# Delta rule and rational MLP on one core: one list of places for every engine and the DMA queue

## The chip, the cores and the metric

The kernel runs on one core of a Trainium2 chip. A core has five engines that run side by side and wait for each other by semaphores: TensorE (PE in the profile, its weight loads PEld), VectorE (DVE), ScalarE (ACT), GpSimd (POOL) and SyncE (SP), which here issues nearly all DMAs. The metric is the device time of one execution in microseconds (us); lower is better.

## The reference

A delta-rule recurrence over 768 steps in 4 batches x 8 heads of width 48 makes y, and a rational MLP is applied to each of its 3072 rows of 384.

```python
# attention: B, H, S, D = 4, 8, 768, 48
k_n = k / (norm(k) + 1e-6)
for t in range(S):
    y[:, :, t] = einsum('bhd,bhde->bhe', q[:, :, t], state)
    v_old = einsum('bhde,bhd->bhe', state, k_n[:, :, t])
    state += beta[:, :, t] * outer(k_n[:, :, t], v[:, :, t] - v_old)
# MLP: x = y as (3072, 384), w_in (384, 2048), w_out (2048, 384)
h = x @ w_in
P = a0 + a1*h + a2*h**2 + a3*h**3
Q = 1 + |b0|*|h| + |b1|*h**2
out = (P / (Q + 1e-6)) @ w_out
```

## The kernel before

**Chunks.** The 768 steps are cut into 12 chunks of 64 (`NCH`). For a chunk, *stages* written as Python generators do the attention: `load_k/q/v` fetch the inputs, `keys` normalizes and transposes k, `kbd` writes it by DMA into a block-diagonal tile, `gram` and `gl` form key products (`g`, sent to DRAM as `gd` and read back in blocks as `gb`), `inverse` inverts triangular blocks on VectorE (`wt`, then `wh`, sent out as `img` and read back as `wc`), `blocks` and `solve` finish the triangular solve (`et`, `ebd`, `wbd`, `pu`, `z`), `next` updates the state `S16`, `outputs` makes y, and `tokens` and `scalars` prepare the scaled rows `xT` and the table `msc` for the MLP. A `yield` ends a *step* of a stage.

**Units.** The MLP is cut into 96 units, 8 for a chunk (`NU`, 256 columns of the 2048 each): `hidden` (18 matmuls into `ph`, L902), `numerator`, `cubic` and `quotient` (six VectorE operations of 128 x 512, L926 to L953, five on ScalarE, one on GpSimd), and `accumulate` (12 matmuls into `po`, L969). The tiles `mx` of the units are a ring of three buffers. The first VectorE operation of `numerator` (L926) marks a unit below. Units 0 to 7 need chunk 0's tokens, units 8 to 15 need chunk 1's, and so on.

**Weights.** `load_in` and `load_out` (8 of each) fetch 768 KB of float64 words into a staging tile (`wsi`, `wso`) and turn them into float32 and then into two float16 parts: ScalarE (L343), GpSimd (L344), three VectorE operations (L345, L347 twice) and more. The staging tiles are of the same ring of three as `mx`, so that a weight's DMA waits until the weight three places earlier has been converted, and unit 0 waits until nearly all weights have been. The `units` 0 to 3 of chunk 0 use the first four weights of each kind, with a scalar table of their own; units 4 to 7 use the others.

**What sets the order.** Each step of a chunk has a time in units (`PLAN`), each step of a unit another (`UNIT`), the same for all chunks and units; the steps are sorted by time. Steps before unit 8 (`upto = 8.0`), the constants and the weights are written in groups (chunk 0, weights 0 to 3, weights 4 to 7, later chunks), and the framework's scheduler, with its own model of time, orders them on every engine. From unit 8 on VectorE, ScalarE, TensorE and GpSimd follow the sorted steps (`manual_schedule`); the SP queue is ordered by the scheduler throughout. Two things hold work back by hand: `gate`, a scalar that is made from the result of chunk 0's inverse (L631) and that the conversions of weights 4 to 7 and of all of `w_out` read on GpSimd (L344), and `BEHIND`, by which some loads are issued after a named DMA.

```python
        nc.gpsimd.tensor_scalar(t.bitcast(F32), t.bitcast(F32), 3.0e38, keep, op0=ALU.min, op1=ALU.max)   # L344, keep = gate
    if upto < N:
        with tc.manual_schedule(engines={DVE, Activation, PE, Pool}):   # L1142, names shortened
```

Of the kernel before, what the change touches and what calls it, by code (L numbers as in the profile page):

```python
# [36 lines left out]
def kernel(  # L37
# [16 lines left out]
    P = 128  # L54
# [39 lines left out]
    marks = {}  # L94
    BEHIND = {"k1": "kbd0", "v1": "kbd0", "q1": "gb0", "k2": "gb0", "v2": "gb0", "q2": "gb0", "knbd0": "gb0"}

    def mark(nm, c, dma):
        marks[f"{nm}{c}"] = dma.ins

    def behind(nm, c):  # L100
        after = marks.get(BEHIND.get(f"{nm}{c}"))
        return nullcontext() if after is None else tc.issue_after(after)

# [6 lines left out]
    for t in wide.values():  # L110
        nc.vector.memset(t[:, :, :, D:], 0.0)

    def load(nm, c):
        t = wide[nm] if nm in wide else sb.tile([P, HP, D], F32, tag="ld" + nm, name=f"{nm}_{c}", bufs=LD_BUFS[nm])
        with behind(nm, c):
            for b in range(2):
                sl, src = slice(b * C, (b + 1) * C), SRC[nm][:, :, c * C : (c + 1) * C]
                if nm == "v":
                    nc.sync.dma_start(out=t[sl], in_=src[2 * b : 2 * b + 2].rearrange("p h t d -> t (p h) d"))
                else:  # L120
                    for i in range(2):
                        nc.sync.dma_start(out=t[sl, :, i, :D], in_=src[2 * i + b].rearrange("h t d -> t h d"))
        loaded[nm, c] = t
# [21 lines left out]
    nc.gpsimd.memset(mask, 1.0 / 256.0)
    for b in range(2):
        sl = slice(b * C, (b + 1) * C)
        nc.gpsimd.affine_select(
            out=mask[sl],
            in_=mask[sl],  # L150
            pattern=[[1, C]],
            compare_op=ALU.is_gt,
            fill=0.0,
            base=0,
            channel_multiplier=-1,
        )
# [15 lines left out]
    bblk = cpool.tile([P, NCH, 16], F32, name="bblk")  # L172
    for j in range(NB):
        nc.scalar.dma_start(
            out=bblk[j:P:NB],
            in_=beta.rearrange("b h (c j i) -> j (b h) c i", j=NB, i=16)[j],
        )

    nc.gpsimd.tensor_scalar(bblk, bblk, 1.0 / 256.0, 0.0, op0=ALU.mult, op1=ALU.add)


    def zeroed(n, shape, dtype, nm, part=lambda t: t, eng=nc.gpsimd):
        made = []
# [24 lines left out]
    NIMG = 2
    img = []
    for i in range(NIMG):  # L210
        t = dfix.tile([P, BS], F32, name=f"img{i}")
        nc.scalar.dma_start(out=t, in_=zero)
        img.append(t)
# [82 lines left out]
    NU = NF // 2  # L296
    w_in = cpool.tile([P, NU, 2, NCC, 2 * P], F16, name="w_in")
# [9 lines left out]
    def tables(lo, hi):  # L307
# [3 lines left out]
        nc.scalar.activation(wn, wn, AF.Exp, scale=0.5, bias=consts[:, 1:2])  # L311
        row = [tab[:, i, u] for i in range(6)]
# [11 lines left out]
        nc.vector.tensor_scalar_mul(io, total(io, hi - lo, f"o{lo}", ps_h, "h"), 2.0 ** -14)  # L324
# [9 lines left out]
    gate = cpool.tile([P, 1], F32, name="gate")  # L334

    def to_f32(t, src, nm, keep=MIN_NORMAL):

        n = t.shape[-1]
        st = staged([P, n, 2], U32, "ws" + nm)
        parts_ = src.shape[1]  # L340
        nc.sync.dma_start(out=st.rearrange("p (a f) w -> p a (f w)", a=parts_), in_=src)
        wl, wh = st[..., 0], st[..., 1]
        nc.scalar.activation(t.bitcast(F32), wh.bitcast(F32), AF.Abs)  # L343
        nc.gpsimd.tensor_scalar(t.bitcast(F32), t.bitcast(F32), 3.0e38, keep, op0=ALU.min, op1=ALU.max)  # L344
        nc.vector.tensor_scalar(t, t, 3, KEEP, op0=ALU.logical_shift_left, op1=ALU.bitwise_and)  # L345
        for word, scalar, op0 in ((wh, 0xC0000000, ALU.bitwise_and), (wl, 29, ALU.logical_shift_right)):
            nc.vector.scalar_tensor_tensor(out=t, in0=word, scalar=scalar, in1=t, op0=op0, op1=ALU.bitwise_or)  # L347

    def load_in(i):
        w64 = moe_w_in.bitcast(U32)
        t = w_out[:, i].rearrange("p a b e -> p (a b e)").bitcast(U32)
        to_f32(
            t, w64[:, i * 4 * P : (i + 1) * 4 * P].rearrange("(c p) x -> p c x", p=P), f"i{i}", gate if i >= 4 else MIN_NORMAL
        )
        t = t.bitcast(F32).rearrange("p (c f) -> p c f", c=NCC)
        s2 = w_in[:, i, 0].bitcast(BF16)
        nc.scalar.activation(s2, t, AF.Square)
        pf = ps_h.tile([P, 2 * P], F32, tag="h", name=f"pfw{i}")  # L360
        for cc in range(NCC):
            nc.tensor.matmul(pf, ones16, s2[:, cc], start=cc == 0, stop=cc == NCC - 1)
        ss = sb.tile([P, 1], F32, tag="ss", name=f"wss_{i}")
        nc.vector.tensor_reduce(sw[:, 2, i : i + 1], pf, axis=AX.X, op=ALU.max)
        nc.vector.tensor_scalar_max(sw[:, 2, i : i + 1], sw[:, 2, i : i + 1], 2.0 ** -60)
        nc.scalar.activation(s2[:, 0], pf, AF.Copy, accum_out=ss)
        nc.vector.tensor_scalar_max(ss, ss, 2.0 ** -2)
        scale_of(sw[:, 0, i : i + 1], ss, f"w{i}")
        split16((w_in[:, i, 0], w_in[:, i, 1]), t, sw[:, 0, i : i + 1])

    def load_out(i):
# [5 lines left out]
        to_f32(t, w64[2 * i * P : (2 * i + 2) * P].rearrange("(j p) x -> p j x", j=2), f"o{i}", gate)  # L377
# [65 lines left out]
    def to_diagonal(nm, t, c=0):  # L443
        bd = diag[nm][c % len(diag[nm])]
        for b in range(2):
# [7 lines left out]
            elif nm in "kq":  # L453
                dma = nc.sync.dma_start(
# [3 lines left out]
                mark(nm + "bd", c, dma)  # L458
# [41 lines left out]
    info = {}  # L500
# [3 lines left out]
    def keys_normalized(c):  # L504

        nrm = sb.tile([P, 4, HP], F32, tag="nrm", name=f"nrm_{c}", bufs=1)
        kt = loaded.pop(("k", c))
# [21 lines left out]
        info[c] = {}  # L529
# [21 lines left out]
    def key_products(c):  # L551
# [3 lines left out]
        mm3(pg, d["kbd"], d.pop("tk"))  # L555
# [616 lines left out]
```

## Time and profile before

| | |
|---|---|
| median of 3 runs (lowest, highest) | 792.67 us (790.21, 793.26) |
| the profiled execution | 790.87 us, span 789.1 us, mean granted TensorE clock 0.925 |
| busy, share of the span | VectorE 712.7 us (90%), ScalarE 661.9 (84%), TensorE 639.4 (81%), GpSimd 313.9 (40%) |
| DMA | 84.35 MB, mean 107 GB/s |

The span runs from the first to the last instruction; 1.8 us of the execution lie around it. Busy time is that in which an engine has at least one operation under way; back-to-back VectorE operations overlap a little, so that the sum of their durations is more. Idle time before an operation is put down to what released it. Times in rows are microseconds from the start of the span. A row of windows gives a stretch, its length, then each engine's busy time in it with the number of instructions, the granted TensorE clock, the mean busy share of the 16 DMA engines and GB/s.

### The profile page before, as it was taken

The numbers are of one execution on the slowest core, as the hardware profiler recorded it, in microseconds if no ns is written. First come the engines' busy times: TensorE is split into PE (matmuls) and PEld (weight loads), VectorE is DVE, ScalarE is ACT, GpSimd is POOL, SyncE is SP. The second block draws the span as 40 slices with busy tenths as digits, with TensorE's granted clock in tenths as the row PEclk, the third lists the DMA queues.
The fourth block names the chain that finished last, engine by engine and source line by source line (L and its number), as shares of the span: only waits on it lengthen the run. The fifth ranks groups of instructions, "written<-read, shape, count | busy, mean of one in ns | idle before, by whom it ended". The sixth has DMA issues, their size and how long they took to land.

```text
span 789.1 us, 23451 instructions
## 1 busy us (share of the span) xinstructions
PE 639.4 (81%) x9520; PEld 510.7 (65%) x9520; DVE 712.7 (90%) x1290; ACT 661.9 (84%) x1301; POOL 313.9 (40%) x321
## 2 busy tenths in 40 slices
PE   0413555768599899899999998999999988999995
PEld 0313544657488778777687787777877876777662
DVE  5698789799679999999999999999999999898996
ACT  3765788988779999999999999999999977887973
POOL 7542356352125436335354353353442342222222
PEclk9955586799599999999999999999999999999999
DMA  8897897747836467286385574772853713400000
GB/s 230 189 187 188 190 197 148 121 82 122 131 61 118 82 120 136 57 151 117 67 146 110 99 132 82 132 135 43 162 95 77 137 26 55 85 2 22 1 21 21
DMA packets 358412, 84.35 MB, mean 107 GB/s; under 512 B 349856, under 2 KB 352928, under 8 KB 358304
## 3 DMA queue, kind: packets, MB, share of 16 engines
q1 hardware_dynamic: 356128, 81.69, 53.7%
q8 instruction: 75, 1.23, 0.7%
q10 hardware_dynamic: 2176, 1.17, 0.5%
q14 instruction: 33, 0.27, 0.1%
HBM read 34.70 MB, written 13.65 MB: 61 GB/s over the span
## 4 chain that ended last, share of the span: by engine, by line
DVE 41%; PE 20%; ACT 6%; DMA 3%; issue 3%; SPq 0%; POOLq 0%; ACTq 0%; DVEq 0%
PE ph L902 8%; DVE ph L951 5%; DVE mg L949 5%; DVE mx L953 4%; PE po L969 4%; DVE mx L936 4%; DVE mx L926 4%; DVE mx L934 4%; DVE z L257 3%; PE py L422 2%; ACT mx L923 2%; PE pm L422 1%; DMA gd<-g 1%; DVE pr L597 1%; DVE pr L616 1%
## 5 line engine op out<-in xcount | busy, mean ns | idle before, releaser
L955 POOL TENSOR_TENSOR mg<-mx 128x512 f16<-128x512 f32 x96 | 129.0, 1344 | 327.5 <-DVE mx L953 175.4
L969 PE MATMUL po<-w_out,mg 128*128 128x384 f16 x1152 | 218.0, 327 | 10.9 <-DVE mg L949 5.7
L902 PE MATMUL ph<-xT,w_in 128*128 128x256 f16 x1728 | 209.1, 276 | 12.2 <-DVE mx L953 8.6
L902 PEld LDWEIGHTS <-w_in 128*128 128x128 f16 x1728 | 167.4, 99 | 44.9 <-DVE mx L953 18.1
L969 PEld LDWEIGHTS <-mg 128*128 128x128 f16 x1152 | 106.3, 98 | 72.1 <-DVE mg L949 10.9
L922 ACT ACTIVATE mx<-ph,msc 128x512 f32<-128x512 f32 x96 | 65.5, 683 | 21.2 <-PE ph L902 19.0
L949 DVE SCALAR_TENSOR_TENSOR mg<-mx,msc 128x512 f16<-128x512 f32 x96 | 75.4, 785 | 1.3 <-ACT mx L945 1.2
L951 DVE SCALAR_TENSOR_TENSOR ph<-mx,msc,mg 128x512 f32<-128x512 f32 x96 | 73.8, 769 | 1.2
L422 PE MATMUL pu<-z,ebd 128*128 128x48 f16 x1728 | 54.3, 188 | 25.1 <-DVE z L257 20.3
L422 PEld LDWEIGHTS <-ebd 128*128 128x128 f16 x1728 | 53.8, 100 | 32.2 <-issue 29.8
L923 ACT ACTIVATE mx<-ph,coef,msc 128x512 f32<-128x512 f32 x96 | 74.4, 775 | 0.0
L422 PEld LDWEIGHTS <-kbd 128*128 128x128 f16 x1680 | 58.9, 103 | 21.9 <-issue 13.5
L953 DVE SCALAR_TENSOR_TENSOR mx<-mx,msc,ph 128x512 f32<-128x512 f32 x96 | 71.2, 742 | 1.6
L934 DVE TENSOR_TENSOR mx<-ph,mx 128x512 f32<-128x512 f32 x96 | 65.5, 682 | 6.4 <-ACT mx L923 6.2
L936 DVE SCALAR_TENSOR_TENSOR mx<-mx,msc,ph 128x512 f32<-128x512 f32 x96 | 71.0, 739 | 0.0
L926 DVE SCALAR_TENSOR_TENSOR mx<-mx,msc,ph 128x512 f32<-128x512 f32 x96 | 70.8, 738 | 0.0
L928 ACT ACTIVATE mx<-mx 128x512 f32<-128x512 f32 x96 | 60.1, 626 | 11.6 <-DVE mx L926 11.6
L943 ACT ACTIVATE mx<-mx,msc 128x512 f32<-128x512 f32 x96 | 68.7, 715 | 0.1
L945 ACT ACTIVATE mx<-mx 128x512 f32<-128x512 f32 x96 | 60.4, 629 | 2.2
L253 POOL TENSOR_TENSOR mm<-m,mm 128x512 f16<-128x512 f32 x24 | 33.9, 1419 | 28.4 <-ACT mm L247 19.2
L255 ACT ACTIVATE z<-pu,zmask 128x768 f16<-128x768 f32 x36 | 32.7, 910 | 11.3 <-PE pu L422 10.6
L422 PEld LDWEIGHTS <-wbd 128*128 128x128 f16 x1152 | 34.3, 99 | 11.0 <-issue 6.7
(197 smaller groups left out, 1228.9 us busy)
## 6 DMA issues: line engine op xcount, KB each, us to landing
wsi<-in_moe_w_in_dram SPq DMA_DIRECT2D x8, 768.0 KB, 7.7
gd<-g SPq DMA_DIRECT2D x24, 256.0 KB, 4.9
wso<-in_moe_w_out_dram SPq DMA_DIRECT2D x8, 768.0 KB, 5.8
mbd<-mm SPq DMA_DIRECT2D x24, 256.0 KB, 4.9
wc<-img SPq DMA_DIRECT2D x24, 256.0 KB, 4.8
wbd<-wc SPq DMA_DIRECT2D x24, 256.0 KB, 5.1
knbd<-kn SPq DMA_DIRECT2D x44, 128.0 KB, 4.3
kw<-in_k_dram SPq DMA_DIRECT2D x48, 96.0 KB, 3.4
```

The source lines that it names most:

```text
L422: nc.tensor.matmul(dst[p][:, h], head(bd, lp, p * H + h), head(rt, rp, p * H + h), start=start and n == 0 and h == 0, stop=stop and n == l ...
L902: nc.tensor.matmul(ph[:, i], w_in[:, f2, wp, cc, i * P : (i + 1) * P], x[:, xp, cc], start=k == 0, stop=k == 3 * NCC - 1,)
L923: nc.scalar.activation(u, ph, AF.Identity, scale=A3, bias=a2)
L926: in_order(nc.vector.scalar_tensor_tensor(out=w, in0=z, scalar=B0, in1=ph, op0=ALU.add, op1=ALU.mult))
L934: in_order(nc.vector.tensor_mul(u, ph, u))
L936: in_order(nc.vector.scalar_tensor_tensor(out=u, in0=u, scalar=A1, in1=ph, op0=ALU.add, op1=ALU.mult))
L943: nc.scalar.activation(r, w, AF.Ln, bias=Q0)
L949: in_order(nc.vector.scalar_tensor_tensor(out=g[:, 0], in0=u, scalar=A0, in1=r, op0=ALU.add, op1=ALU.mult))
L951: in_order(nc.vector.scalar_tensor_tensor(out=t, in0=w, scalar=Q0, in1=g[:, 0], op0=ALU.add, op1=ALU.mult))
L953: in_order(nc.vector.scalar_tensor_tensor(out=u, in0=u, scalar=A0, in1=t, op0=ALU.add, op1=ALU.subtract))
L955: nc.gpsimd.tensor_mul(g[:, 1], u, r)
L969: nc.tensor.matmul(po[p], g[:, gp, i, p * P : (p + 1) * P], w_out[:, f2, wp, i], start=f2 == lo and i == 0 and k == 0, stop=f2 == hi - 1 a ...
```

## The change

The table of times, the scheduler's part, the gate and `BEHIND` go. Every step of every stage, for each chunk, unit, weight, constant and zeroed buffer by itself, gets a place in one list of 2996 (`PLACES`); `run` walks the list once, and `manual_schedule()` without arguments makes all engines and the SP queue follow it. To this end the constants, the zeroing of buffers, the weights' conversion and the tables have become stages with steps of their own; `weights` i and the scalars of units 0 to 3 and 4 to 7 can stand anywhere among the chunks' steps. The arithmetic is the same, but for the gate's two operands and one constant tile (`ident16`) that nothing read.

```diff
-    BEHIND = {"k1": "kbd0", "v1": "kbd0", "q1": "gb0", "k2": "gb0", "v2": "gb0", "q2": "gb0", "knbd0": "gb0"}
...
-        with behind(nm, c):
-            for b in range(2):
+        for b in range(2):
...
-    gate = cpool.tile([P, 1], F32, name="gate")
-    def to_f32(t, src, nm, keep=MIN_NORMAL):
+    def to_f32(t, src, nm):
...
+        yield
         nc.scalar.activation(t.bitcast(F32), wh.bitcast(F32), AF.Abs)
-        nc.gpsimd.tensor_scalar(t.bitcast(F32), t.bitcast(F32), 3.0e38, keep, op0=ALU.min, op1=ALU.max)
+        yield
+        nc.gpsimd.tensor_scalar(t.bitcast(F32), t.bitcast(F32), 3.0e38, MIN_NORMAL, op0=ALU.min, op1=ALU.max)
+        yield
...
-        if c == 0:
-            nc.vector.tensor_scalar(
-                gate.bitcast(U32), wtf[:, 127:128].bitcast(U32), 0, 897 << 20, op0=ALU.bitwise_and, op1=ALU.bitwise_or
-            )
...
-    PLAN = {
-        "load_k": (-32.4564,),
...
+    PLACES = {
+        "weights_in": (
+            (1, 2, 10, 11, 14, 21, 58, 67, 70, 85, 86, 107, 118, 121, 126),
...
-    for e in early:
-        if e[2] == 0 and e[1] != "hidden":
-            do(e)
-    weights(0, GRP)
-    tables(0, GRP)
-    scalars(0, 0, GRP)
-    weights(GRP, NU)
...
-        with tc.manual_schedule(engines={mybir.EngineType.DVE, mybir.EngineType.Activation, mybir.EngineType.PE, mybir.EngineType.Pool}):
-            for e in events:
-                if e[0] >= upto:
-                    do(e)
+    def run(places):
+        stages = {}
+        for _, nm, n in sorted((x, nm, n) for nm, rows in places.items() for n, row in enumerate(rows) for x in row):
+            if (nm, n) not in stages:
+                stages[nm, n] = STAGES[nm](n) or iter(())
+            next(stages[nm, n], None)
+    with tc.manual_schedule():
+        run(PLACES)
```

Three places show the move. In the rows below `kw`, `qw` and `v` are the loads of a chunk's k, q and v, `wsi` and `wso` those of a weight of `w_in` and `w_out`, and the other names are the tiles told above.

The first DMAs of the SP queue, before:

```order
L122 DMA kw<-in_k_dram 64x8x48 x4
L122 DMA qw<-in_q_dram 64x8x48 x4
L119 DMA v_158<-in_v_dram 64x16x48 x2
L341 DMA wsi_781<-in_moe_w_in_dram 128x3x512
L341 DMA wsi_804<-in_moe_w_in_dram 128x3x512
L341 DMA wsi_827<-in_moe_w_in_dram 128x3x512
L454 DMA kbd_123<-tk_177 48x16x128 x2
L122 DMA kw<-in_k_dram 64x8x48 x3
```

and in the changed kernel:

```order
L301 DMA wsi_112<-in_moe_w_in_dram 128x3x512
L107 DMA kw<-in_k_dram 64x8x48 x4
L107 DMA qw<-in_q_dram 64x8x48 x4
L104 DMA v_159<-in_v_dram 64x16x48 x2
L301 DMA wsi_177<-in_moe_w_in_dram 128x3x512
L301 DMA wsi_217<-in_moe_w_in_dram 128x3x512
L301 DMA wsi_219<-in_moe_w_in_dram 128x3x512
L107 DMA kw<-in_k_dram 64x8x48 x4
L428 DMA kbd_93<-tk_192 48x16x128 x2
L301 DMA wsi_235<-in_moe_w_in_dram 128x3x512
```

The first weight goes from the fourth to the first place, and the loads of k, q and v of chunk 0 one place back; a fourth and a fifth weight follow around chunk 1's k.

The SP queue around the last of the 16 weights, before:

```order
L449 DMA knbd_129<-kn_117 64x8x128 x3
L454 DMA qbd_127<-tq_1295 48x16x128 x2
L122 DMA kw<-in_k_dram 64x8x48 x4
L462 DMA mbd_135<-mm_1389 64x16x128 x2
L454 DMA kbd_123<-tk_1391 48x16x128 x2
L637 DMA img_141<-wh_1435 128x16x16
L642 DMA wc_1517<-img_141 64x16x64 x2
L341 DMA wso_1133<-in_moe_w_out_dram 128x2x768
L561 DMA gd_1439<-g_1494 64x16x64 x2
L119 DMA v_1786<-in_v_dram 64x16x48
```

and in the changed kernel:

```order
L301 DMA wso_781<-in_moe_w_out_dram 128x2x768
L301 DMA wso_785<-in_moe_w_out_dram 128x2x768
L107 DMA kw<-in_k_dram 64x8x48 x4
L428 DMA kbd_94<-tk_788 48x16x128 x2
L423 DMA knbd_96<-kn_89 64x8x128 x4
L301 DMA wso_958<-in_moe_w_out_dram 128x2x768
L104 DMA v_969<-in_v_dram 64x16x48 x2
L533 DMA gd_1038<-g_1097 64x16x64 x2
L423 DMA knbd_96<-kn_90 64x8x128 x4
L547 DMA gb_1172<-gd_1038 128x16x16
```

The last weight (`wso_1133`, now `wso_958`) goes from place 55 to place 39 of the queue: chunk 1's `gd`, `gb`, `qbd`, `mbd`, `img` and `wc`, which stood ahead of it, stand behind it now; chunk 0's `knbd` and chunk 1's `kbd` stay ahead of it.

VectorE around the first operation of unit 0 (L926 before, L888 now; its `mx` is written), before:

```order
L280 TENSOR_SCALAR sw<-lgw_1089 128x1
L257 SCALAR_TENSOR_TENSOR et_1574<-pe_1523,et_1574 128x768
L385 TENSOR_TENSOR vss_1087<-sw 128x1
L240 SCALAR_TENSOR_TENSOR w_out<-w_out,vss_1087 128x768
L881 TENSOR_TENSOR msc_1007<-tab,sf_761 128x6x4
L345 TENSOR_SCALAR wo_7_1132<-wo_7_1132 128x768
L526 RECIPROCAL nrm_1505<-nrm_1505 128x16
L382 TENSOR_SCALAR vss_1105<-wfs_1103 128x1
L347 SCALAR_TENSOR_TENSOR wo_7_1132<-wso_1133,wo_7_1132 128x768
L934 TENSOR_TENSOR mx_2079<-ph_2055,mx_2079 128x512
L347 SCALAR_TENSOR_TENSOR wo_7_1132<-wso_1133,wo_7_1132 128x768
L926 SCALAR_TENSOR_TENSOR mx_2079<-mx_2079,msc_1007,ph_2055 128x512
```

and in the changed kernel:

```order
L278 SCALAR_TENSOR_TENSOR tab<-sw,coef 128x4
L279 SCALAR_TENSOR_TENSOR tab<-tab,sw 128x4
L280 TENSOR_SCALAR tab<-tab,coef 128x4
L282 RECIPROCAL sw<-sw 128x4
L236 TENSOR_SCALAR sc_1424<-lgq_1489 128x2
L847 TENSOR_TENSOR msc_1599<-tab,sf_1314 128x6x4
L217 SCALAR_TENSOR_TENSOR w_out<-wo_7_957,vss_1548,w_out 128x768
L888 SCALAR_TENSOR_TENSOR mx_1601<-mx_1601,msc_1599,ph_1580 128x512
L896 TENSOR_TENSOR mx_1601<-ph_1580,mx_1601 128x512
L660 RECIPROCAL sc_947<-sc_947 128x2
L898 SCALAR_TENSOR_TENSOR mx_1601<-mx_1601,msc_1599,ph_1580 128x512
L888 SCALAR_TENSOR_TENSOR mx_1626<-mx_1626,msc_1599,ph_1604 128x512
```

Before, unit 0 starts between the conversions of the last weight (`wo_7`), and the last scaled parts of `w_out` follow later. Now all 16 weights are finished and unit 0's operations and unit 1's stand together. The row of unit 0 is number 220 of VectorE's list in both.

More of the change, by code (lines that the diff above doesn't have):

```diff
@@ L140 @@
-    ones16 = sb.tile([P, P], BF16, tag="xT", name="ones16")
-    nc.gpsimd.memset(ones16, 1.0)
+    ones16 = cpool.tile([P, P], BF16, name="ones16")
     mask = cpool.tile([P, C], F32, name="mask")
[L145 to L156, printed above, removed]
@@ L208 @@
[L208 to L213, printed above, removed]
+    LN2 = math.log(2.0)
+    kn_b = [cpool.tile([P, 2, 2, NH, DP, HG], F16, name=f"kn{i}") for i in range(3)]
+    wt_b = [cpool.tile([P, 272], F32, name="wt0")]
+    diag = {nm: [cpool.tile(SHAPE[nm], F16, name=f"{nm}bd{i}") for i in range(2 if nm == "k" else 1)] for nm in SHAPE}
+    BS = 16 * C + 16
+    NIMG = 2
+    img = [dfix.tile([P, BS], F32, name=f"img{i}") for i in range(NIMG)]
@@ new lines, with zeros, stage @@
+    filled = {}
+    def zeros(nm):
+        def stage(i):
+            if nm == "img":
+                if not i:
+                    filled[nm] = sb.tile([P, BS], F32, tag="ob", name="zero", bufs=1)
+                    nc.gpsimd.memset(filled[nm], 0.0)
+                    yield
+                for t in img:
+                    nc.scalar.dma_start(out=t, in_=filled[nm])
+                return
+            if nm == "rows":
+                t = kn_b[i][:, :, :, :, D:DP]
+            else:
+                t = wt_b[i] if nm == "wt" else diag[nm][i]
+            eng = nc.vector if nm in ("k", "w", "e", "rows") else nc.gpsimd
+            eng.memset(t if nm == "wt" else t.bitcast(F32), 0.0)
+            yield
+        return stage
@@ L498, in transposed @@
         d[to] = t
-    info = {}
+    info = [{} for _ in range(NCH)]
     fmax = {}
@@ L715, in rows_to_diagonal @@
         d = info[c]
-        with behind("knbd", c):
-            d["knbd"] = to_diagonal("kn", d.pop("kd"))
+        d["knbd"] = to_diagonal("kn", d["kd"])
         yield
@@ L1078 @@
     }
-    def of_chunk(c):
-        for nm, times in PLAN.items():
-            if c == 0 and nm in ("state", "qbd", "scalars") or c == NCH - 1 and nm in ("rows", "knbd", "next"):
-                continue
-            if c == 0 and nm == "residual":
-                times = times[2:]
-            made = []
-            for i, t in enumerate(times):
-                yield NU * c + t, nm, c, i == len(times) - 1, made
-    def of_unit(n):
-        for nm, times in UNIT.items():
-            made = []
-            for i, t in enumerate(times):
-                yield n + t, nm, n, i == len(times) - 1, made
@@ L1098, in do @@
-    def do(event):
-        t, nm, n, last, made = event
-        if not made:
-            made.append(STAGES[nm](n) or iter(()))
-        with tc.high_priority(FIRST[nm]) if nm in FIRST else nullcontext():
-            if last:
-                run(made[0])
-            else:
-                next(made[0], None)
-    events = [e for c in range(NCH) for e in of_chunk(c)] + [e for n in range(N) for e in of_unit(n)]
-    events.sort(key=lambda e: e[0])
-    GRP = 4
-    def weights(lo, hi):
-        for i in range(lo + (lo > 0), min(hi + 1, NU)):
-            load_in(i)
-        for i in range(lo, hi):
-            load_out(i)
```

1094 lines of the change are left out of this document (921 added, 173 removed), and 86 rows, old and new, of the table PLACES.

## The prediction

> **What bounds the kernel now.** I read the page's first two parts, then windows by stage, then who waits in each stage, then the SP queue in order of time.
>
> ```profile
> span 789.1 us, 23451 instructions
> ...
> PE 639.4 (81%) x9520; PEld 510.7 (65%) x9520; DVE 712.7 (90%) x1290; ACT 661.9 (84%) x1301; POOL 313.9 (40%) x321
> ...
> DVE  5698789799679999999999999999999999898996
> ...
> q1 hardware_dynamic: 356128, 81.69, 53.7%
> ```
>
> VectorE is busy for 712.7 of 789.1 us and near full from a quarter of the span on; 76.4 us of it are idle. The list moves its work and takes away two small operations, so the time is about 712 us plus what idle time the new order leaves. The windows say where the 76.4 us lie: length less DVE.
>
> ```profile
> 0.00:34.00 34.00, 9.01 (x76) 7.31 (x77) 20.15 (x30) 16.79 (x32) 22.36 (x36) 1.00 0.81 197
> 34.00:145.00 111.00, 51.85 (x784) 43.38 (x784) 92.62 (x194) 83.31 (x187) 49.99 (x51) 0.60 0.88 185
> 145.00:200.00 55.00, 40.01 (x747) 34.09 (x745) 47.91 (x108) 46.88 (x102) 22.27 (x25) 0.93 0.60 104
> 200.00:221.00 21.00, 13.23 (x205) 11.10 (x205) 11.37 (x21) 12.80 (x28) 2.57 (x2) 0.59 0.68 107
> 221.00:231.00 10.00, 10.00 (x130) 7.78 (x129) 9.70 (x15) 9.25 (x17) 1.69 (x2) 1.00 0.26 45
> 231.00:632.00 401.00, 377.41 (x6012) 305.25 (x6007) 389.74 (x697) 373.80 (x723) 171.01 (x173) 1.00 0.59 110
> 632.00:762.00 130.00, 119.81 (x1462) 90.48 (x1461) 122.00 (x204) 105.70 (x199) 36.08 (x29) 0.99 0.16 32
> 762.00:789.20 27.20, 18.08 (x122) 11.26 (x122) 19.25 (x27) 13.39 (x22) 7.98 (x6) 0.97 0.06 15
> ```
>
> Idle: 13.9 and 18.4 up to unit 0 (32.2), then 7.1, 9.6 and 0.3 up to unit 8 (17.0), 11.3 in the 401 us of full work, 8.0 and 8.0 at the end. In the first 145 us the DMA engines are 0.81 to 0.88 busy at 185 to 197 GB/s: here two resources are nearly full. Afterwards DMA is not (0.6).
>
> ```profile
> 18.67 0.88 ACT L343 ACTIVATE w_out<-wsi 128x768 f32<-128x768 f32 x1
> 19.89 0.83 POOL L344 TENSOR_SCALAR w_out<-w_out 128x768 f32<-128x768 f32 x1
> 20.75 0.56 DVE L345 TENSOR_SCALAR w_out<-w_out 128x768 uint32<-128x768 uint32 x1 [6.36 <-POOL w_out L344]
> 58.58 2.34 POOL L344 TENSOR_SCALAR w_out<-w_out,gate 128x768 f32<-128x768 f32 x2 [5.33 <-DVE gate L631]
> 140.22 0.55 DVE L345 TENSOR_SCALAR wo<-wo 128x768 uint32<-128x768 uint32 x1
> 144.75 0.74 DVE L926 SCALAR_TENSOR_TENSOR mx<-mx,msc,ph 128x512 f32<-128x512 f32 x1
> 212.52 1.81 PE L422 MATMUL pg<-tk,kbd 128*128 128x64 f16 x31 [3.01 <-DMA kbd<-tk]
> 219.71 0.69 ACT L922 ACTIVATE mx<-ph,msc 128x512 f32<-128x512 f32 x1 [3.91 <-PE ph L902]
> 221.16 0.69 DVE L934 TENSOR_TENSOR mx<-ph,mx 128x512 f32<-128x512 f32 x1 [4.54 <-ACT mx L923]
> 230.94 0.73 DVE L926 SCALAR_TENSOR_TENSOR mx<-mx,msc,ph 128x512 f32<-128x512 f32 x1
> 631.90 0.74 DVE L926 SCALAR_TENSOR_TENSOR mx<-mx,msc,ph 128x512 f32<-128x512 f32 x1
> ```
>
> These rows are instructions: start, duration, idle time before; those of L926 are the first operations of units 0, 8 and 68. VectorE gets its first weight at 20.75; the gate makes GpSimd wait at 58.58; the last weight is converted at 140.22, and unit 0 follows at 144.75 because the ring of three gives it no buffer earlier. At 212 to 221, where the hand-ordered part begins, TensorE stands for a DMA of `kbd` with unit 6's matmuls queued behind; ScalarE and then VectorE wait in turn.
>
> ```profile
> 0.80 2.88 SPq L122 DMA_DIRECT2D kw<-in_k_dram  x4
> 9.24 4.20 SPq L341 DMA_DIRECT2D wsi<-in_moe_w_in_dram  x3
> 23.20 1.41 SPq L454 DMA_DIRECT2D kbd<-tk  x2
> 39.09 2.56 SPq L575 DMA_DIRECT2D gb<-gd  x1
> 72.76 6.27 SPq L658 DMA_DIRECT2D ebd<-et  x6
> 130.01 0.38 SPq L341 DMA_DIRECT2D wso<-in_moe_w_out_dram  x1
> ...
> wsi<-in_moe_w_in_dram SPq DMA_DIRECT2D x8, 768.0 KB, 7.7
> ...
> wso<-in_moe_w_out_dram SPq DMA_DIRECT2D x8, 768.0 KB, 5.8
> ```
>
> The SP queue issues the first weights at 9.24 and the last at 130.01; one lands 5.8 to 7.7 us after issue.
>
> **The change part by part.** I take each stretch's idle time in turn.
>
> *To 34 us.* Issued first (0.8), weight 0 lands near 8.5 (7.7 later) and, with 0.88 and 0.83 us on ScalarE and GpSimd, reaches VectorE near 10.5 and not 20.75. That doesn't bring 10 us: k of chunk 0 is issued one DMA later (1.4 us, a third of 4.20), so `kbd` goes out near 24, as before (23.20), and SP must wait there for chunk 1's k too, whose norm stands among the conversions on VectorE. Following the list, four weights' three operations, the memsets and two norms, 22.3 us of work by the durations of their rows, are done by about 34 us, where before it was 20.15. Idle 11.7, a gain of 2.
>
> *34 us to unit 0.* Without the gate a weight waits only for its ring. By rows counted in the list, VectorE has 116 us of work ahead of unit 0 (before 112.8; all of `w_out` is scaled now, one part of it unit 0's own), and 92 ahead of the last weight. With 11.7 idle it comes to that weight at 104 us. Is the weight there? Ahead of it in the SP queue stand 15 weights (11.8 MB), chunk 0 (the queue's 81.69 MB less 12.6 of weights, by 12, is 5.8 MB a chunk; chunk 0 has no `qbd` and its output is later, 5.0), four loads and a `kbd` of later chunks (2.0), and the zeroed images (1.1): 19.8 MB, 104 us at 190 GB/s. It lands near 110 and VectorE waits some 6 us. The ends: 0, if the weights' large packets run above the mean rate, and the old 18.4, if SP stands. I take 6, since both resources come out at the same 104 us. Unit 0 starts at 134 (116 + 17.7), not 144.75.
>
> *Unit 0 to unit 8.* The hand-over at 200 to 221 (9.6) goes, as there is one order and no change of regime: SP, which runs ahead in the list, has chunk 4's `kbd` well ahead of its product, though chunk 3's stands next to it. The 7.1 us between 145 and 200 are chains of chunks 1 and 2 that remain. Between units 0 and 4 the list has 46 us of VectorE's work and 1.25 chunks of DMA (rows counted); a chunk is 8 of the 60 units between 231 and 632, 53.5 us at a DMA share of 0.59 or 32 us, so 40 us of DMA, tighter than before (55 us at 0.60). I take 5; ends 2 and 12.
>
> *Units 8 to 68.* The unit-by-unit VectorE order is nearly the old one: at units 16, 32 and 68 the work ahead differs by less than 2 us. What waits there is small.
>
> ```profile
> DVE xs L814 <- PE px L812: 5.6, 8, 0.7
> ```
>
> This row, of 231 to 632, is half of the idle 11.3: eight waits of 0.7 us for a transpose in `tokens`. The list puts other steps between them, and makes irregular gaps elsewhere. I take 10; ends 4 and 25.
>
> *The end.* From 632 to 762 no attention is left to fill gaps: 8.0, I take 7. The last 8.0 are the chain after the last VectorE operation (GpSimd, matmuls, copy, store), in the list as before: 8.
>
> Sum: 11.7 + 6 + 5 + 10 + 7 + 8 = 47.7 idle, with 712.4 of work 760, and 1.8 around the span (790.87 less 789.1): 762 us. The profiled execution is 0.2% under the median of the runs shown (792.67), so 762 is against either within that.
>
> **The rivals.** *SP stands in order* (0.20). Before, the scheduler chose what SP issued next; now a DMA whose data isn't ready holds all behind it.
>
> ```profile
> SPq L454 <- ACT w_out L343: 10.0, 1, 10.0
> ```
>
> Before, SP stood 10.0 us for the first `kbd`. In the list six `ebd` (6.27 us of issue) are ahead of the last three weights, and k of chunk 2, `kbd` of chunk 1 and `knbd` of chunk 0 ahead of the last. If 34 us to unit 0 keeps its 18.4 and the next stretch takes 10, the time is 762 + 12.4 + 5 = 779. For it speaks that weights are what unit 0 waits for; against, that the last weight has 16 fewer places ahead. The Trainium skill, "DMA: Bandwidth & Descriptors", section "Anatomy of one DMA — SWDGE (gpsimd) path", says the same of the mechanism: DMA engines do not wait on semaphores, the issuing sequencer does, before it dispatches. The 10.0 us row agrees; it is a rule that speaks against a fixed SP order, and by it this rival's 779 would be the forecast.
>
> *The full stage gets slower* (0.08). In the 401 us each `gram` on TensorE waits for `kbd`.
>
> ```profile
> PE pg L422 <- DMA kbd<-tk: 14.4, 4, 4.4
> ```
>
> Four such waits cost 14.4, 4.4 the longest. Before, SP's order there followed the scheduler's estimate; an out-of-place store or load ahead of `kbd` in the list stops TensorE, and units' matmuls behind it, for up to 4.4 us in a chunk. To end over 796 it takes 34 us on my sum, eight late chunks of twelve: 797. Against it: DMA is only 0.59 busy there.
>
> *Nothing is gained* (0.07): VectorE has the same work, and data arrive no earlier; what the start saves is waited for at the recurrence of chunks 1 to 3. 789.
>
> *Better than the sum* (0.10): starting idle 10 and 1, then 3, 5, 6 and 8: 33, so 747.
>
> The forecast holds 0.55, for 750 to 774.
>
> **How the numbers follow.** About 0.5% (4 us) is what a measurement can tell from no change. Faster: 0.55 + 0.10 + 0.20 = 0.85; the same 0.07; slower 0.08. The range leaves out the slower case and part of the better: 747 to 785.
>
> **What would show it.** Right: the last weight converted near 110, unit 0 at 128 to 138, unit 8 near 205 (before 231), no stretch like 200 to 221, 9 to 14 us idle in the full stage. SP rival: waits on SP ahead of `wso` after 80 us, unit 0 after 140. Slower rival: `pg` waits for `kbd` in many chunks and VectorE under 95% between units 8 and 68. The sum is wrong if VectorE's operations themselves get longer, which busy time over 720 us would show.

## The result, and the profile after

| | median, lowest to highest | ratio to before, 95% interval |
|---|---|---|
| before | 791.44 us, 789.35 to 793.26, 4 runs | |
| the list | 765.53 us, 765.14 to 768.66, 4 runs | 0.9682, 0.9644 to 0.972 |

The list is 25.9 us faster by the medians. The profiled execution took 765.28 us, with a span of 763.6. From its page: the span, each engine's busy time, VectorE's 40 slices, and the chain of waits that ended last, by engine.

```profile
span 763.6 us, 23465 instructions
...
PE 629.3 (82%) x9520; PEld 506.6 (66%) x9520; DVE 691.9 (91%) x1288; ACT 661.1 (87%) x1301; POOL 311.7 (41%) x321
...
DVE  6789988867898999898998999999989999999995
...
DVE 32%; ACT 25%; PE 20%; DMA 10%; issue 5%; SPq 3%; POOL 2%; ACTq 0%; DVEq 0%; POOLq 0%
```

Before, slices 11 and 12 were at 6 and 7, the hole of 200 to 221 us; now slices 9 and 10 are (153 to 191 us). The hole has moved and not closed. And look at VectorE's sum: 691.9 us and not 712.7, for the same arithmetic. Its idle time is 763.6 less 691.9, 71.7 us, and was 76.4. So 20.8 us of the gain are *shorter work* and only 4.7 less waiting. The windows, cut where the list's units start (length, then busy time of TensorE, its weight loads, VectorE, ScalarE and GpSimd, the granted clock, DMA share, GB/s):

```profile
0.00:34.00 34.00, 6.51 (x59) 5.23 (x60) 24.02 (x30) 17.56 (x34) 24.70 (x37) 1.00 0.82 188
34.00:135.00 101.00, 43.43 (x705) 37.04 (x703) 89.25 (x203) 84.27 (x183) 39.20 (x45) 0.66 0.96 190
135.00:190.00 55.00, 43.23 (x897) 36.88 (x895) 41.62 (x94) 47.54 (x99) 23.88 (x28) 0.99 0.77 126
190.00:214.60 24.60, 20.04 (x248) 15.72 (x248) 22.37 (x40) 22.01 (x44) 7.37 (x6) 0.80 0.65 111
214.60:613.00 398.40, 379.47 (x6034) 309.03 (x6032) 375.84 (x694) 370.81 (x723) 172.75 (x173) 0.98 0.67 111
613.00:736.30 123.30, 116.82 (x1460) 89.95 (x1457) 120.57 (x208) 106.03 (x201) 36.06 (x29) 1.00 0.20 38
736.30:763.60 27.30, 19.81 (x136) 12.79 (x134) 18.25 (x27) 12.91 (x21) 7.79 (x6) 0.99 0.06 15
```

Length less VectorE gives the idle time: 10.0, 11.8, 13.4, 2.2, 22.6, 2.7, 9.1. Between units 8 and 68 VectorE has 13.9 us less work than before (375.84 against 389.74), yet the stretch is only 2.6 us shorter (398.4 against 401.0), because its idle time doubled from 11.3 to 22.6. The milestones, as single instructions (start, duration, idle time before):

```profile
0.80 0.45 SPq L301 DMA_DIRECT2D wsi<-in_moe_w_in_dram  x1
...
98.42 0.59 SPq L301 DMA_DIRECT2D wso<-in_moe_w_out_dram  x1
...
106.84 1.82 DVE L308 TENSOR_SCALAR wo<-wo 128x768 uint32<-128x768 uint32 x1 [1.82 <-POOL wo L306]
134.82 0.75 DVE L888 SCALAR_TENSOR_TENSOR mx<-mx,msc,ph 128x512 f32<-128x512 f32 x1 [0.53 <-ACT mx L885]
214.55 0.75 DVE L888 SCALAR_TENSOR_TENSOR mx<-mx,msc,ph 128x512 f32<-128x512 f32 x1
613.02 0.72 DVE L888 SCALAR_TENSOR_TENSOR mx<-mx,msc,ph 128x512 f32<-128x512 f32 x1
```

SP issues the first weight at 0.80 (9.24 before) and the last at 98.42 (130.01). Its conversion starts at 106.84 (140.22), and units 0, 8 and 68 at 134.82, 214.55 and 613.02, so 9.9, 16.4 and 18.9 us earlier than before.

**Where the work went.** First three rows from the timeline of before, in the full stage; then one from the list; then the two groups that lost most, before and after (count, busy us, mean ns).

```profile
278.22 0.32 DVE L626 TENSOR_SCALAR wh<-wt 128x256 f16<-128x256 f32 x1
278.47 1.27 POOL L955 TENSOR_TENSOR mg<-mx 128x512 f16<-128x512 f32 x1 [4.15 <-ACT sf L849]
278.57 1.48 DVE L627 SCALAR_TENSOR_TENSOR wh<-wt,wh 128x256 f16<-128x256 f32 x1
...
L627 DVE SCALAR_TENSOR_TENSOR wh<-wt,wh 128x256 f16<-128x256 f32 x12 | 13.7, 1141 | 0.3
L597 DVE TENSOR_TENSOR pr<-wt,ab 128x4 f32<-128x4 f32 x12 | 10.8, 900 | 0.3
```

```profile
262.81 0.45 DVE L598 SCALAR_TENSOR_TENSOR wh<-wt,wh 128x256 f16<-128x256 f32 x1
...
L598 DVE SCALAR_TENSOR_TENSOR wh<-wt,wh 128x256 f16<-128x256 f32 x12 | 5.4, 450 | 0.4
L568 DVE TENSOR_TENSOR pr<-wt,ab 128x4 f32<-128x4 f32 x12 | 2.0, 165 | 0.6
```

The operation `wh<-wt,wh` takes 0.45 us. Before, it began at 278.57, 0.10 us after GpSimd's `mg`, and lasted until that was over: `mg` ends at 279.74, and the wh operation at 280.05, after 1.48 us. Most of that time is a wait, but it is counted as busy. It met `mg` so in 8 of 12 chunks, because the table of times put it right behind a unit's last VectorE operation; the small product `pr` met GpSimd's `mm` in 9 of 12. In the list neither meets anything. By their rows the two groups lose 17.1 us.

### The profile page after: what moved, and what is told of

The parts are those of the page before. It is cut to its first block, busy times and chain, and to the rows that moved or that the text cites. A ratio compares the mean times of both kernels' runs of the same rounds, so it can differ in the third digit from the quotient of the medians.

```text
span 763.6 us, 23465 instructions
## 1 busy us (share of the span) xinstructions
PE 629.3 (82%) x9520; PEld 506.6 (66%) x9520; DVE 691.9 (91%) x1288; ACT 661.1 (87%) x1301; POOL 311.7 (41%) x321
## 2 busy tenths in 40 slices
DMA packets 358412, 84.35 MB, mean 110 GB/s; under 512 B 349856, under 2 KB 352928, under 8 KB 358304
## 4 chain that ended last, share of the span: by engine, by line
DVE 32%; ACT 25%; PE 20%; DMA 10%; issue 5%; SPq 3%; POOL 2%; ACTq 0%; DVEq 0%; POOLq 0%
PE ph L864 7%; PE po L931 5%; DVE mx L888 3%; ACT mx L885 3%; DVE ph L913 3%; ACT mx L884 3%; DVE mx L915 3%; DVE mx L896 3%; DVE mg L910 3%; DVE mx L898 3%; ACT kp L815 2%; DVE w_out L311 2%; PE pu L396 2%; ACT mx L904 2%; ACT mx L890 2%
## 5 line engine op out<-in xcount | busy, mean ns | idle before, releaser
L917 POOL TENSOR_TENSOR mg<-mx 128x512 f16<-128x512 f32 x96 | 129.7, 1351 | 277.2 <-DVE mx L915 167.5
L931 PE MATMUL po<-w_out,mg 128*128 128x384 f16 x1152 | 214.5, 329 | 4.3 <-POOL mg L917 2.4
L864 PE MATMUL ph<-xT,w_in 128*128 128x256 f16 x1728 | 205.1, 273 | 10.9 <-DVE mx L915 9.3
L864 PEld LDWEIGHTS <-w_in 128*128 128x128 f16 x1728 | 165.6, 98 | 41.0 <-DVE mx L915 9.3
L931 PEld LDWEIGHTS <-mg 128*128 128x128 f16 x1152 | 109.5, 99 | 65.8 <-POOL mg L917 3.1
L910 DVE SCALAR_TENSOR_TENSOR mg<-mx,msc 128x512 f16<-128x512 f32 x96 | 73.3, 764 | 2.7 <-ACT mx L906 2.6
L888 DVE SCALAR_TENSOR_TENSOR mx<-mx,msc,ph 128x512 f32<-128x512 f32 x96 | 70.7, 737 | 1.9 <-issue 1.1
L396 PEld LDWEIGHTS <-ebd 128*128 128x128 f16 x1728 | 51.2, 98 | 15.6 <-issue 11.4
L396 PE MATMUL pu<-z,ebd 128*128 128x48 f16 x1728 | 52.0, 186 | 11.4 <-DVE z L217 10.1
L213 POOL TENSOR_TENSOR mm<-m,mm 128x512 f16<-128x512 f32 x24 | 31.6, 1328 | 34.4 <-ACT mm L207 28.1
L217 DVE SCALAR_TENSOR_TENSOR z<-pu,zmask,z 128x768 f16<-128x768 f32 x36 | 36.4, 1011 | 5.7 <-ACT z L215 5.7
```

Source lines behind the costliest of these rows:

```text
L396: nc.tensor.matmul(dst[p][:, h], head(bd, lp, p * H + h), head(rt, rp, p * H + h), start=start and n == 0 and h == 0, stop=stop and n == l ...
L864: nc.tensor.matmul(ph[:, i], w_in[:, f2, wp, cc, i * P : (i + 1) * P], x[:, xp, cc], start=k == 0, stop=k == 3 * NCC - 1,)
L888: nc.vector.scalar_tensor_tensor(out=w, in0=z, scalar=B0, in1=ph, op0=ALU.add, op1=ALU.mult)
L910: nc.vector.scalar_tensor_tensor(out=g[:, 0], in0=u, scalar=A0, in1=r, op0=ALU.add, op1=ALU.mult)
L917: nc.gpsimd.tensor_mul(g[:, 1], u, r)
L931: nc.tensor.matmul(po[p], g[:, gp, i, p * P : (p + 1) * P], w_out[:, f2, wp, i], start=f2 == lo and i == 0 and k == 0, stop=f2 == hi - 1 a ...
```

## The experiments

Each time is given with its ratio to the kernel before, run beside it. Differences between two changed kernels are taken from these ratios, at 791 us, and half-intervals are in us.

**Which stretch carries the gain.** Three kernels take the list for some stretches and the old table of times for the rest, on all engines and SP; a cut is at the named unit's first step.

```diff
-        for _, nm, n in sorted((x, nm, n) for nm, rows in places.items() ...):
+        SEGMENTS = (("new", 8), ("old", None))          # start_new
+        SEGMENTS = (("new", 68), ("old", None))         # start_and_full_new
+        SEGMENTS = (("new", 8), ("old", 68), ("new", None))   # full_old
+        for order, unit in SEGMENTS:
+            for x, nm, n in new if order == "new" else old:
+                if unit is not None and (nm, n) == ("numerator", unit):
+                    break
...
```

> The list up to unit 8's first step, and from there the old table of times, on all engines. Theory A, each stretch keeps its own gain: the two traces differ by 16.3 us at unit 8, so 791.4 - 16.3 = 775 us (771 to 779), with unit 8 near 215. Theory B, the stretches lean on each other (the old order after unit 8 counts on steps that stand elsewhere in the start): part of the 16 us is lost again soon after unit 8, 780 us or more.

Measured: 776.59 us, ratio 0.9826 (0.981 to 0.9843), unit 8 at 217.8. Theory A.

> The list up to unit 68, then the old table of times. Theory A: the traces differ by 2.6 us more at unit 68, so about 772 us (769 to 776), and units 68 to 92 take about 130 us as before, not 123.3. Theory B, that the last part is short because the chunk work of the full stage has been moved ahead of it: it stays at 123 to 125 us with the old order too, and the time is 766 to 768.

Measured: 772.62 us, ratio 0.9794 (0.9766 to 0.9822). Units 68 to 92 in this kernel and then in the list:

```profile
612.50:742.20 129.70, 118.77 (x1466) 89.97 (x1465) 121.60 (x204) 105.79 (x199) 34.68 (x28) 1.00 0.19 36
```

It is 129.7 us against the list's 123.3, with 1.0 us more work and 5.4 us more idle time: Theory A again, the end's gain is that of its own order. Of the list's 25.2 us (1 less 0.9682, of 791) the start to unit 8 is worth 13.8 (half-interval 1.3), the full stage 2.5 (2.6), and the rest 8.9 (3.7). So the full stage's part is not clear of nothing, and why the list's own order ends faster isn't shown.

> The list, but units 8 to 68 by the old table of times. Theory A, VectorE sets the full stage and its order matters through the operations that meet a GpSimd operation: VectorE's busy time of units 8 to 68 goes back up by about 13.8 us, and of that the time rises by the 2.6 us that the traces differ by, 768 us (766 to 771). Theory C, the 13.8 us of shorter operations are worth their length, and something else in the new order loses 11: then the time rises by more where the old order lacks the other's losses, or falls below 765, outside 766 to 771.

Measured: 771.3 us, ratio 0.9765 (0.975 to 0.9781), 6.6 us (half-interval 3.3) over the list. The full stage in its trace:

```profile
220.40:620.20 399.80, 375.76 (x6028) 304.16 (x6026) 388.12 (x693) 373.32 (x719) 168.86 (x171) 1.00 0.64 110
```

VectorE's work is up by 12.3 us, as both theories had it, and the stretch by 1.4. So 11 us of the shorter operations are indeed given back there as idle time. That the time rose by 6.6 and not 2.6 I can't place for sure: in this trace unit 8 comes at 220.4, but in the seven other traces that share the start's list (one of them with two steps moved) it comes at 213.4 to 217.8, so one look at the start is good to some 3 us either way.

**Is it SP's order or the engines'?** One kernel keeps the list on four engines and leaves SP to the scheduler; the next does the reverse.

```diff
-    with tc.manual_schedule():
+    with tc.manual_schedule(engines={DVE, Activation, PE, Pool}):   # sp_free
+    with tc.manual_schedule(engines={SP}):                          # sp_only
```

> The list for TensorE, VectorE, ScalarE and GpSimd, word for word; the order of the SP queue is left to the scheduler, as before. Theory A, the SP queue's place in the list doesn't matter, since what its DMAs wait for is on the engines: 764 to 770 us. Rival (SP stands in order): a DMA that waits holds the ones behind it in the list, and freeing the queue takes 10 us or more off, 755 or less. Third: the list's SP order is itself a gain, and with the scheduler's order the start or the chunks' products wait: over 772.

Measured: 794.32 us, ratio 1.0061 (1.0036 to 1.0086). The third case, and far beyond it: with the engines' orders word for word the same, the SP order alone costs 30 us (half-interval 3.6), all of the gain and more. From its trace: windows of the start, of units 0 to 8 and of the full stage; the SP queue's issue of `knbd` and of the last weight and its conversion; and waits between units 8 and 68.

```profile
34.00:146.60 112.60, 46.56 (x695) 39.28 (x693) 87.40 (x202) 84.35 (x183) 38.41 (x44) 0.61 0.76 166
146.60:234.80 88.20, 66.29 (x1145) 54.78 (x1143) 64.06 (x132) 69.93 (x143) 30.88 (x34) 0.86 0.66 111
234.80:642.50 407.70, 379.98 (x6037) 309.38 (x6035) 375.61 (x694) 371.11 (x723) 172.75 (x173) 0.99 0.64 109
...
28.68 4.38 SPq L423 DMA_DIRECT2D knbd<-kn  x4
102.76 1.06 SPq L301 DMA_DIRECT2D wso<-in_moe_w_out_dram  x1
118.84 1.82 DVE L308 TENSOR_SCALAR wo<-wo 128x768 uint32<-128x768 uint32 x1 [0.66 <-POOL wo L306]
...
ACT y L759 <- DMA out_dram<-ob: 11.5, 7, 3.5
PE pk L396 <- ACT y L759: 11.0, 6, 3.2
DVE v L717 <- PE pk L396: 10.2, 5, 3.3
```

VectorE's work is the same as in the list (375.61 against 375.84 in the full stage): the loss is all waiting. In the start the scheduler's estimate sends `knbd` of chunk 0 and loads of later chunks out ahead of weights; the last weight is converted 12.0 us later, and unit 0 follows 27.8 us behind it, as in the list (28.0); from there to unit 8 it takes 88.2 us, and 79.6 in the list. In the full stage ScalarE waits for the buffer of the output's store before it can write `y`, TensorE's `pk` for `y`, and VectorE's `v` for `pk`: the last three rows are one chain, and VectorE's end of it is worth 10.2 us; the stage is 9.3 us longer than the list's. SP issues these stores 1.8 to 2.7 us after their data are complete in five of the stage's eight chunks (411.5 and 414.1, for one), behind other DMAs; in the list it is 0.1 us or less in all eight.

> The complement of the run before: the SP queue's order is the list's, word for word, and TensorE, VectorE, ScalarE and GpSimd are left to the scheduler, with no gate. Theory D, the order of the SP queue alone carries the gain, since in the start the DMA engines are what everything waits for: 765 to 775 us, unit 0 at 134 to 138. Rival E, SP's order and the engines' order are only good together, since SP then waits in order for results that the engines give in another order: over 785 us, with waits of SP longer than the list's 5.7 us.

Measured: 888.69 us, ratio 1.1236 (1.1199 to 1.1272). Rival E, by its time and by SP's waits. The full stage, and SP's longest waits over the span (us in total, times, longest):

```profile
244.30:718.00 473.70, 402.38 (x5944) 324.20 (x5941) 394.73 (x700) 365.98 (x708) 170.37 (x161) 0.94 0.56 92
...
SPq L957 <- ACT ob L948: 99.3, 3, 41.2
SPq L428 <- ACT sf L815: 86.3, 4, 25.3
SPq L957 <- ACT mx L890: 34.8, 3, 30.3
SPq L428 <- PE py L396: 30.3, 3, 21.1
```

SP stands up to 25 us in the full stage for a result that ScalarE gives late, with the next chunks' DMAs behind it (`kbd` and `qbd` are issued at L428), and up to 41 us for the output near the end (L957). This is the prediction's rival "SP stands in order", at full size: the fixed queue doesn't agree with the engines' order. How much of the loss is the scheduler's own engine order, which here also holds from unit 8 on, isn't shown: no kernel left both to the scheduler.

> The kernel before without its gate and without its rules on what SP may not issue earlier (BEHIND); all else as before. Theory A, gate and rules cost: GpSimd's 5.33 us wait for the gate goes and the weights come earlier, 784 to 788 us, and a part of the gain is theirs. Theory D, they mended the scheduler's SP order: without them loads and knbd go out ahead of chunk 0's kbd, gd and gb and of weights, as in the run with SP left to the scheduler, unit 0 comes at 147 or later and the time is 795 us or more.

```diff
-    BEHIND = {"k1": "kbd0", "v1": "kbd0", "q1": "gb0", ...}
+    BEHIND = {}
-        nc.gpsimd.tensor_scalar(t.bitcast(F32), t.bitcast(F32), 3.0e38, keep, ...)
+        nc.gpsimd.tensor_scalar(t.bitcast(F32), t.bitcast(F32), 3.0e38, MIN_NORMAL, ...)
```

Measured: 794.24 us, ratio 1.0044 (1.0024 to 1.0063), unit 0 at 149.6. In direction Theory D, at the edge of its number: gate and rules together were mending the scheduler's order and were worth 3.5 us (half-interval 1.5). Taken away by themselves, with the operation that makes the gate, they give no part of the gain.

**Is VectorE's work the bound of the full stage?** Two kernels make or unmake the meetings of `wh` with GpSimd, three add work to one engine each.

```diff
-            (460, 484, 485, 491, 495, 507, 516, 534, 572, 575),     # wh_meets_gpsimd, and so for chunks 3 to 10
+            (460, 484, 485, 491, 495, 507, 516, 540.1, 572, 575),
-        "inverse": (..., -17.7935, -16.8416, -16.3475, -14.0101),   # before_wh_clear
+        "inverse": (..., -17.7935, -16.45, -16.3475, -14.0101),
+        if 8 <= n < 68: nc.vector.memset(extra, 0.0)                 # vector_more, in numerator
+        if 8 <= n < 68: two matmuls into ph[:, 0], start and stop    # tensor_more, in hidden
+        if 8 <= n < 68: nc.scalar.copy(extra[:, 128:216], extra[:, :88])   # scalar_more, in numerator
```

> The list with one VectorE step (the split of the inverse, wh) moved by 1 to 21 places in chunks 2 to 10, so that it stands behind a unit's last VectorE operation, where GpSimd has just begun mg. Each of the nine second operations should take 1.48 us and not 0.45, as in the kernel before: VectorE busy 692 + 9 = 701 us. Theory T1, VectorE's busy time sets the full stage: 9 us more, 774 to 776. Theory T2, another engine or a chain does, and VectorE has room there: 764 to 768.

Measured: 777.53 us, ratio 0.9829 (0.9797 to 0.9861), 11.6 us (half-interval 3.9) over the list.

```profile
L598 DVE SCALAR_TENSOR_TENSOR wh<-wt,wh 128x256 f16<-128x256 f32 x12 | 13.6, 1130 | 0.4
217.80:629.70 411.90, 384.24 (x6036) 311.45 (x6035) 385.08 (x694) 371.37 (x723) 172.27 (x173) 0.97 0.64 107
```

Eight of the twelve met `mg`, by their place alone (a mean of 1130 ns, where the list has 450). The full stage has 9.2 us more work and is 13.5 longer: T1's side, and more than its sum. The step moved by up to 17 places, later in seven chunks and earlier in two, and the chain behind it (`img`, `wc`) with it, so this run doesn't price the meeting by itself.

> The kernel before with one number changed: the wh step of every chunk 0.39 unit later, behind the cubic's last VectorE operation, where GpSimd's mg is over. The eight operations of 1.48 us become 0.45, VectorE busy 712.7 - 8.2 = 704.5 us. Theory T1: 782 to 784 us. Theory T2: within 2 us of before, 788 to 791.

Measured: 785.73 us, ratio 0.9936 (0.9911 to 0.9961), 5.1 us (half-interval 2.0) under before.

```profile
L627 DVE SCALAR_TENSOR_TENSOR wh<-wt,wh 128x256 f16<-128x256 f32 x12 | 5.4, 450 | 0.3
229.30:626.80 397.50, 377.62 (x6012) 305.61 (x6008) 383.11 (x697) 373.60 (x723) 170.64 (x173) 1.00 0.61 111
```

One number of the old table clears all meetings with `mg` (a mean of 450 ns, 1141 before). The full stage loses 6.6 us of VectorE's work and 3.5 of its length: between T1 and T2, about half.

> The list with one operation more on VectorE in each of the units 8 to 67: a memset of 128x256 of a spare buffer, 0.272 us by the row of kw, right behind the unit's first operation; 60 x 0.272 = 16.3 us, and nobody reads it. Theory T1, VectorE's own work sets the full stage: 14 to 18 us more, 780 to 783. Theory T2, it has room (22.6 us idle in these 398.4): 0 to 6 us more. Theory T3, the chain through a unit (VectorE, ScalarE, VectorE, TensorE in turn) sets it, whichever engine is lengthened: about the same sum as for the other two engines.

Measured: 771.99 us, ratio 0.9765 (0.9739 to 0.9792), 6.6 us (half-interval 3.7) over the list.

```profile
L891 DVE MEMSET extra<- 128x256 f32 x60 | 16.3, 272 | 0.2
216.55:619.85 403.30, 381.32 (x6038) 308.75 (x6036) 385.34 (x753) 372.44 (x723) 173.16 (x173) 0.99 0.66 109
```

Of the 16.3 us only 9.5 add to VectorE's busy time, as neighbours overlap them or are recorded shorter, and of these 4.9 to the stage: about half, as in the run before. The time is just over T2's range and far below T1's.

> The list with two matmuls more in each of the units 8 to 67, ahead of the unit's first product, which they repeat (1075 of them took 127.7 us, 0.119 us each): 120 x 0.119 = 14.3 us of TensorE. T1: 0 to 4 us more, 765 to 770, though TensorE is 95% busy there. T2 with TensorE as the bound: 12 to 16 more, 777 to 782. T3: about as much as the VectorE run.

> The list with one operation more on ScalarE in each of the units 8 to 67: a copy of 128x88 between spare buffers, some 0.27 us (between 0.309 for 128 columns and 0.68 for 512), behind the unit's first one, ahead of the one that TensorE's next product doesn't need but VectorE's cubic does: 16 us of ScalarE. T1: 0 to 4 us more. T2 with ScalarE as the bound (27.6 us idle there): 12 or more. T3: about as much as the VectorE run.

Measured: 766.84 us, ratio 0.9701 (0.9677 to 0.9726), and 767.26, ratio 0.9697 (0.9677 to 0.9718): 1.5 and 1.2 us over the list, within the intervals. The full stage of the two, TensorE's run first:

```profile
213.43:611.43 398.00, 387.57 (x6153) 319.62 (x6152) 376.93 (x694) 371.80 (x723) 172.32 (x173) 0.99 0.66 111
215.98:614.89 398.91, 380.10 (x6035) 308.44 (x6032) 376.14 (x693) 378.02 (x782) 172.81 (x173) 0.99 0.66 110
```

Like VectorE's, their busy time rose by less than the sum of what was added: TensorE's by 8.1 us and ScalarE's by 7.2, and the stage is 0.4 us shorter and 0.5 longer than the list's. So TensorE, 95% busy in the list's stage, and ScalarE, 93%, have room where the work was added. VectorE's run is 5.1 and 5.4 us over these two (half-intervals 2.9 and 2.6): of the three engines only VectorE has a price that shows, some half a microsecond for one of busy time. T3 is out.

**Is the start held by the DMA engines?**

```diff
+        if nm in ("i4", "i5", "i6"):
+            x = dfix.tile([DM, 4 * P], U32, name="x" + nm)
+            nc.sync.dma_start(out=x, in_=moe_w_in.bitcast(U32)[:, : 4 * P])
```

> The list with three transfers more in the start, each of 768 KB from the weights in memory to a spare place in memory, issued by SP right behind the weights 4 to 6 of the first kind; nobody reads them. 2.36 MB at the 190 GB/s of the start are 12.4 us. Theory, the DMA engines set the start (their share is 0.96 from 34 to 135 us): unit 0 comes 8 to 13 us later, 774 to 779. Rival, VectorE's work and its chains set it: unit 0 within 3 us of 134.8, 764 to 769.

Measured: 766.94 us, ratio 0.9692 (0.9677 to 0.9706), 0.8 us over the list, within the intervals. In its trace the window of the start, and the last weight's conversion:

```profile
34.00:135.00 101.00, 40.31 (x671) 34.32 (x669) 88.45 (x202) 80.94 (x179) 38.79 (x45) 0.64 0.98 211
...
110.17 1.82 DVE L311 TENSOR_SCALAR wo<-wo 128x768 uint32<-128x768 uint32 x1 [1.65 <-POOL wo L309]
```

Unit 0 came at 140.0 in this trace, 5.1 us later than in the list's and beyond the 133.6 to 138.3 of the eight other traces with this start: between the two forecasts. The time is the rival's. The engines carried 211 GB/s at a share of 0.98, where the list had 190 at 0.96: the rate in bytes is no ceiling. But the run added some 1200 packets, of about 2 KB, to 358412 of 235 bytes on average. Whether the many small packets hold the DMA engines, which are busy for 0.96 of the stretch, isn't tested.

## Why the prediction was right, and where not

The time was right (762 forecast, 765.53 measured), and so was its sign and its largest event: one order puts the weights ahead. That its sum came out is luck: two terms were wrong by nearly the same amount. Work was to be 712.4 and was 691.9, 20.5 less; idle time was to be 47.7 and was 71.7, 24.0 more.

- *"VectorE has the same work."* This step failed. I took busy time as work. 17.1 us in two groups alone were waits behind GpSimd inside operations, visible before as one shape at two durations (443 to 1491 ns for `wh`). The list's order removes them and adds others: the weights' shift (L345, now L308) rose from a mean of 583 ns to 939. The prediction named the opposite sign only (busy over 720).
- *To 34 us*: 11.7 forecast, 10.0 measured.
- *34 us to unit 0*: 6 forecast, 11.8 measured. The last weight near 110 (106.8 measured) and unit 0 at 134 (134.8) held, and so did the 24 us of work behind the last weight: 23.5, with 4.5 idle. What failed is the reason for the 6: 19.8 MB at 190 GB/s as a limit. VectorE waited 1.82 us for the last weight, and 2.36 MB more in the same stretch cost 0.8 us in the time, not 12.4. What the rows show in its place is the ring: the weights wait for their staging buffers to be converted (SP stood 17.4 us for that in the list, eight times, longest 3.8).
- *Unit 0 to unit 8*: 5 forecast, 15.6 measured, unit 8 at 214.6 and not near 205. The wait of 200 to 221 is gone, as said, but the idle time only moved, to 154 to 192, around the scalar chain, the solve and the state of the next chunks. The longest waits of VectorE there are for four different reasons:

```profile
DVE nrm L499 <- POOL nrm L497: 2.7, 1, 2.7
DVE z L213 <- ACT z L207: 2.2, 1, 2.2
DVE v L717 <- PE pk L396: 1.5, 1, 1.5
DVE S L744 <- PE pd L396: 1.5, 1, 1.5
```

 None of the four is released by a DMA. The chain of waits that ended last does pass through DMA landings near there, though: `img` of 5.10 us at 124.58, `wc` of 6.12 at 130.35 and `gb` of 6.61 at 139.43, then `gd` of 4.33 at 168.03 and `kbd` of 4.99 at 189.48. So a DMA's share in this idle time isn't excluded. The step "the hand-over goes" priced the hole as the cause; by these rows I read it as a place where the slack of the chunks' chains showed, which no run here tests.

- *Units 8 to 68*: 10 forecast, 22.6 measured, outside my 9 to 14. The eight waits of 0.7 for `xs` are down to two, 1.0 us in all, but irregular ones came, as the waits of these 398 us show:

```profile
DVE z L217 <- ACT z L215: 4.8, 4, 2.4
DVE xT L217 <- ACT xT L215: 3.6, 2, 3.3
DVE mg L910 <- ACT mx L906: 2.4, 1, 2.4
DVE ab L564 <- DMA gb<-gd: 2.2, 1, 2.2
```

 That a good part of the work which leaves VectorE comes back as idle time is what the runs showed: a half (before_wh_clear, and vector_more the other way), four fifths (before against the list), nine tenths (full_old against the list). Only wh_meets_gpsimd, whose chain was moved as well, lost more than its work.
- *The end*: 7 and 8 forecast, 2.7 and 9.1 measured. The first was taken nearly as before (8.0); start_and_full_new shows that the list's order there is worth about 6 us of the span.
- *The rivals.* "SP stands in order" didn't come in the list, because its SP order and its engine orders agree; sp_only shows it real, and sp_free shows what I had not priced at all, that leaving SP to the scheduler costs more: 30 us. The Trainium skill, "DMA: Bandwidth & Descriptors", section "Anatomy of one DMA — SWDGE (gpsimd) path", has the sequencer wait and not the DMA engines. SP's rows agree (17.4 us for staging buffers in the list, 99.3 for the output in sp_only), but the 779 that I drew from it was wrong: the list has such waits and was 26 us faster. As I read the two runs, a wait on SP costs only if something late is queued behind it. "The full stage gets slower" had a true mechanism in sp_free (9.3 us), by the output's store and not by `kbd`.

What isn't settled: which dependence turns half of VectorE's saved work into waits, why full_old lost 6.6 us where its stage lost 1.4, what makes the end shorter, and whether a fourth staging buffer would bring unit 0 forward; none of that was tried.

## What to carry to other kernels

Before a sum of busy time is used as work, look at each shape's shortest and longest duration: one that lies at two values may be waiting inside, and here a single number of the schedule (before_wh_clear) gave 5 us by moving it off GpSimd's operation. Order the DMA queue together with the engines: either half of this list alone gave 794 and 889 us, both together 766, where the kernel before has 791. When idle time between chains is what you remove, expect a part of it to move and not to go (17.0 us between units 0 and 8 became 15.6). And test a suspected bound by adding to it, and read how much busy time really came: 9.5 us more on VectorE cost 6.6, while 8.1 on TensorE, 7.2 on ScalarE or 2.4 MB of DMA in large packets cost no more than the intervals.

## What was not expected of the hardware

A VectorE operation with two inputs in SBUF (`wh`, `pr`) that starts while GpSimd works in SBUF lasts until GpSimd is done: 1.48 us for 0.45, 1.12 for 0.165. The other four `wh` of before began 0.13 to 0.34 us ahead of a GpSimd operation and took 0.44 to 0.46. An operation that reads PSUM and one SBUF tile, `z`, doesn't: beside an `mg` of 1.27 us at 264.06 in the list, `z<-pu,z` at 264.47 took 0.95 us, its mean over the stage. The Trainium skill, "SBUF — State Buffer", section "SBUF: two separate sides", says that the two engines share a pair of ports as an exclusive lock, which whoever comes first holds for a whole instruction, and counts VectorE operations with two SBUF inputs among those that take it; all of these rows agree. It isn't only operations with two inputs: the one-input shift of the last weight's words (128x768, uint32) took 1.82 us at 106.84, with a GpSimd operation of 1.47 from 106.77, against 0.50 for the weight before it, at 102.11.
